# Where GpSimd writes the low words' integers while weights are converted: back into the raw chunk, or into two buffers of their own

## The chip, the core and the metric

The kernel runs on one core of a Trainium2 chip. It is measured in device microseconds from launch to end; the time shown is the median of three runs. One more execution was taken by the hardware profiler, and its times and trace are what the profile shows. Here TensorE (PE) multiplies matrices and writes to PSUM, VectorE (DVE) and ScalarE (ACT) work on PSUM and SBUF, GpSimd (POOL) works on SBUF, and SyncE (SP) issues most of the DMAs.

## The reference

Attention in which only keys within tau of each row's maximum count, then a feed-forward layer with a squared ReLU. Eight batches of eight heads, 576 rows, head size 64; the result is read as 4608 rows of 512.

```python
def _attn_ref(q, k, v, tau):                       # (8, 8, 576, 64) each, tau = 0.02
    scores = np.matmul(q, k.transpose(0, 1, 3, 2)) / np.sqrt(q.shape[-1])
    thresh = np.max(scores, axis=-1, keepdims=True) - tau
    scores = np.where(scores >= thresh, scores, -1000000000.0)
    scores = scores - np.max(scores, axis=-1, keepdims=True)
    attn = np.exp(scores)
    attn = attn / (np.sum(attn, axis=-1, keepdims=True) + 1e-09)
    return np.matmul(attn, v).astype(np.float32)

def _moe_ref(x, w_in, w_out):                      # (4608, 512), (512, 2048), (2048, 512)
    h = np.maximum(x @ w_in, 0.0)
    return (h * h @ w_out).astype(np.float32)
```

Queries, keys and values come as float32. The two weights come as float64, since they are drawn as float32 and then multiplied by a float64 scalar. The kernel multiplies in float32, so it converts the weights itself, and that is the work which the change touches.

## The kernel before

The kernel has three stages: attention (to about 510 us), the hidden layer and the output layer. Both layers multiply with 49 products of blocks in place of 64, from sums of blocks that VectorE and GpSimd make (the helpers at lines 121 to 125).

**Attention in periods.** The 32 pairs of heads are cut into 144 units of 128 query rows (`units`), and `period(p)` starts two of them, A = 2p and B = 2p + 1, while older ones are finished: the probabilities of period p - 1 are turned by TensorE and the outputs of period p - 2 multiplied with the values and sent out. Each unit has two heads, 0 and 1. The order of instructions in a period is written out by hand, in a list of steps; each engine works through its own instructions in the order in which the list gives them, and waits on semaphores for those of others. The steps that matter here, with the lines at which their instructions stand:

- VectorE: `topA0`, `topA1`, `topB0`, `topB1` (L452) copy a unit's scores from PSUM to SBUF and keep each row's maximum (the scores are negated, so it is a minimum); `maskA0` to `maskB1` (L467) compare the scores with the threshold, multiply with the exponentials and sum, and read two SBUF operands; `inv` (L477) makes reciprocals. The instructions named DVE_READ_ACCUMULATOR in the profile belong to the maxima and masks and write the row's number.
- GpSimd: `leastA` and `leastB` (L459) make a unit's thresholds from its maxima, 128x2 numbers; `over` (L474) and `xm` (L669) are small steps for the row sums and the outputs.
- ScalarE: `powA0` to `powB1` (L462) make the exponentials; `eU`, `eV`, `eW` (L523) and `eT` (L403, L411) copy what TensorE turned out of PSUM.

So a unit's mask waits for its threshold, which waits for both of its maxima.

**Weights in chunks.** 32 chunks of 128x512 float64 numbers (16 of the first weight and 16 of the second) are converted in periods 2 to 34, one chunk begun in each of periods 2 to 33 and finished in the one after. While this goes on the list `CONVERTING` gives the order:

```python
    CONVERTING = """
        s1 fetch SA T U c1 topA1 topA0 leastA eU SB over topB0 PV c2 powA1 powA0 maskA1
        powB0 topB1 c4 eT inv x V powB1 leastB maskA0 maskB0 c3 c5 eV W maskB1 c6 xm eW
    """.split()
```

On VectorE this makes the row topA1, topA0, topB0, maskA1, topB1, c4, inv, maskA0, maskB0, c5, maskB1, and on GpSimd leastA, over, c2, leastB, c3, c6, xm.

`fetch` brings a chunk by DMA into one of four raw buffers of 128x1024 32-bit words: each float64 is a low word and a high word beside each other, so `lo` and `hi` (`pick`) are views of every second word. The conversion then goes in six steps. `c1` (L205, ScalarE) takes the high words' absolute values as bits into a buffer `a`, one of three. `c2` (L212, GpSimd) multiplies the low words, read as unsigned integers, by 2^-29 and writes them as rounded integers from 0 to 8: the top three bits of the low word, rounded. `c3` (L219, GpSimd) bounds `a` to the range of exponents that float32 has. In the next period `c4` (L227, VectorE) shifts `a` by three bits, `c5` (L235, VectorE) joins it with the sign and the top of the exponent in `hi`, and `c6` (L245, GpSimd) adds the integers from `lo`; its result is the float32, written to the weights' tile for the first 16 chunks and to `a`, from where a DMA takes it to DRAM, for the others.

**Where the buffers lie.** One SBUF tile, `arena`, of 27264 float32 a partition is cut by hand. `Region` gives out places in a stretch of it: `tile` takes the next free stretch for a tag seen for the first time and turns round in its ring of buffers after that; `ring` sets the places of a tag by hand. The conversion's region `cv` is the last 6272 words of the arena, of which raw (4 x 1024) and `a` (3 x 512) take 5632; the first layer's input is loaded over it from period 40 on. The pieces of the second weight that are not among the 32 chunks would be converted later, by `convert_out`; with `EARLY` at 16 there are none.

Of the kernel before, what the change touches and what calls it, by code (L numbers as in the profile page):

```python
# [10 lines left out]
FP32 = mybir.dt.float32  # L11
I32 = mybir.dt.int32
U32 = mybir.dt.uint32
ALU = mybir.AluOpType
# [34 lines left out]
def kernel(  # L49
# [25 lines left out]
    nc = tc.nc  # L75
    B, H, S, D = q.shape
    P = 128
# [7 lines left out]
    BANK = 512  # L85
# [13 lines left out]
    ARENA = 27264  # L99
    X_SIZE = 7 * BANK + 3 * 7 * P  # L100
    X_AT = (ARENA - X_SIZE, ARENA - 2 * X_SIZE)
    arena = ctx.enter_context(tc.tile_pool(name="arena", bufs=1)).tile([P, ARENA], FP32, name="arena")
    sb, cv = Region(arena, 0, X_AT[0]), Region(arena, X_AT[0], ARENA)

    ident = const.tile([P, P], FP32, name="ident")
    make_identity(nc, ident)
# [46 lines left out]
    WC = 512  # L153
# [19 lines left out]
    raws, parts = {}, {}  # L173
# [34 lines left out]

    def convert2(m):
        if m in parts:  # L210
            lo = parts[m][0]
            nc.gpsimd.tensor_scalar(out=lo, in0=lo.bitcast(U32), scalar1=2.0**-29, scalar2=None, op0=ALU.mult)  # L212

    def convert3(m):
        if m not in parts:
# [403 lines left out]
    def period(p):  # L619
# [67 lines left out]
        def every(key):  # L687
# [7 lines left out]
            "SA": scored_a, "SB": scored_b,  # L695
            "PV": PV, "x": values_out, "xm": given_out,
            "c1": lambda: convert1(begun(p)), "c2": lambda: convert2(begun(p)),
            "c3": lambda: convert3(begun(p)), "c4": lambda: convert4(begun(p - 1)),
            "c5": lambda: convert5(begun(p - 1)), "c6": lambda: convert6(begun(p - 1)),
# [317 lines left out]
    with tc.manual_schedule():  # L1017
# [54 lines left out]
        def convert_out(n, tick):  # L1072
# [3 lines left out]
            for j, (i, (m, k, h)) in enumerate(mine):  # L1076
# [15 lines left out]
                if step == 0:  # L1092
                    b = b_pool.tile([P, BANK], FP32, tag="b", name="cw")[:, 0 : BANK // 2]
                    nc.scalar.activation(out=b, in_=hi.bitcast(FP32), func=AF.Abs)
                    parts[key] = (lo, hi, b.bitcast(I32))
                    convert2(key)
# [142 lines left out]
```

## Time and profile before

| | |
|---|---|
| runs | 1315.64, 1312.66, 1314.08 us; median 1314.08 |
| profiled execution | 1311.95 us, of which its span (first to last instruction) 1310.2 us |
| TensorE, whole span | 1265.7 us busy (97%) |
| VectorE | 1010.9 us (77%) |
| ScalarE | 845.5 us (65%) |
| GpSimd | 915.6 us (70%) |
| granted TensorE clock, mean | 0.997 |

The shares are means over stages that differ. In attention VectorE is nearly always busy, in the two layers TensorE. The conversion's own rows, over the whole run:

| step | engine, line | times | mean us of one |
|---|---|---|---|
| c1 | ScalarE L205 | 32 | 0.725 |
| c2 | GpSimd L212 | 32 | 2.064 |
| c3 | GpSimd L219 | 32 | 0.626 |
| c4 | VectorE L227 | 32 | 0.417 |
| c5 | VectorE L235 | 32 | 0.682 |
| c6 | GpSimd L245 | 16 + 16 | 1.477 and 1.478 |

The first c2 starts at 24.6 us and the last at 252.3 us; the last c6 starts at 263.5 us. After that the periods go on in the other order (`PLAIN`) to about 510 us. A row of the timeline gives start, length, engine, line, operation, and what is written and read with its shape; idle time of the engine just before it stands in brackets, with what ended it.

### The profile page before, as it was taken

How to read it: one execution, taken by the hardware profiler on the slowest of the kernel's cores; microseconds unless marked ns; L12 is line 12 of the kernel's file. 1: busy time of each engine (PE TensorE's matmuls, PEld its weight loads, DVE VectorE, ACT ScalarE, POOL GpSimd, SP SyncE). 2: the span in 40 equal slices, each digit the busy share in tenths (PEclk: the TensorE clock that was granted, in tenths of full speed). 3: DMA queues.
4: the chain of work that ended last, by engine and by line, in shares of the span. 5: the costliest groups of instructions: out<-in, count | busy, mean ns of one | idle time of the engine just before them, and what ended most of it. 6: DMA issues, size and time to landing. Idle time of an engine off the chain costs nothing.

```text
span 1310.2 us, 47769 instructions
## 1 busy us (share of the span) xinstructions
PE 1265.7 (97%) x19463; PEld 1140.1 (87%) x19463; DVE 1010.9 (77%) x2431; ACT 845.5 (65%) x1498; POOL 915.6 (70%) x1023
## 2 busy tenths in 40 slices
PE   8888888899999999999999999999999999999998
PEld 5666666677777777999999999999999999999998
DVE  6999999999999996877787778777646654665463
ACT  6999999888999985567756775665524332433240
POOL 2777777765555321877887888768777777777775
PEclk8999999999999999999999999999999999999999
DMA  6565666544433312466656665569644225522411
GB/s 159 140 158 138 165 176 192 143 103 98 98 78 83 79 42 62 142 199 193 203 176 202 207 193 170 189 242 395 241 161 162 60 104 161 162 64 99 161 33 34
DMA packets 247035, 192.12 MB, mean 147 GB/s; under 512 B 97184, under 2 KB 195488, under 8 KB 246816
## 3 DMA queue, kind: packets, MB, share of 16 engines
q1 hardware_dynamic: 245504, 188.66, 47.8%
q8 instruction: 153, 2.51, 0.8%
q14 instruction: 66, 0.54, 0.1%
q10 hardware_dynamic: 1312, 0.41, 0.1%
HBM read 116.65 MB, written 72.35 MB: 144 GB/s over the span
## 4 chain that ended last, share of the span: by engine, by line
PE 78%; ACT 4%; DVE 3%; DMA 1%; issue 1%; POOL 1%; ACTq 0%; DVEq 0%; POOLq 0%
PE ph L840 30%; PE po L975 27%; PE sc L532 7%; PE sc L434 6%; PE pt L380 4%; DVE arena L452 2%; PE sc L398 1%; ACT arena L523 1%; ACT arena L462 1%; PE sc L515 1%; DMA wall<-w 1%; DMA arena<-g 0%; DVE arena L125 0%; PE sc L380 0%; DVE arena L122 0%
## 5 line engine op out<-in xcount | busy, mean ns | idle before, releaser
L125 POOL TENSOR_TENSOR arena<-arena 128x512 f32<-128x512 f32 (+1 forms) x314 | 377.8, 1222 | 132.7 <-DVE arena L125 114.7
L975 PE MATMUL po<-wall,arena 128*128 128x128 f32 x3528 | 395.0, 275 | 1.5 <-ACT arena L752 1.4
L975 PEld LDWEIGHTS po<-wall,arena 128*128 128x128 f32 x3528 | 394.3, 192 | 2.1 <-ACT arena L752 1.8
L840 PE MATMUL ph<-arena,wall 128*128 128x128 f32 x3528 | 394.2, 275 | 0.7 <-DVE arena L659 0.7
L840 PEld LDWEIGHTS ph<-arena,wall 128*128 128x128 f32 x3528 | 394.0, 192 | 0.8 <-issue 0.8
L125 DVE TENSOR_TENSOR arena<-ph,arena 128x512 f32<-128x512 f32 x378 | 256.2, 688 | 86.4 <-PE ph L840 65.8
L122 POOL TENSOR_TENSOR arena<-arena 128x128 f32<-128x128 f32 (+2 forms) x314 | 255.2, 814 | 50.4 <-DMA arena<-w 34.2
L467 DVE SCALAR_TENSOR_TENSOR arena<-arena 128x576 f32<-128x576 f32 x288 | 239.6, 853 | 8.4 <-POOL arena L459 6.7
L125 DVE TENSOR_TENSOR arena<-po,arena 128x128 f32<-128x128 f32 x378 | 108.1, 289 | 167.8 <-PE po L975 163.5
L532 PEld LDWEIGHTS sc<-arena 64*64 64x64 f32 x5760 | 153.9, 133 | 82.3 <-DVE arena L452 68.7
L452 DVE TENSOR_SCALAR_CACHE_REDUCE arena<-sc 128x576 f32<-128x576 f32 x288 | 207.3, 747 | 10.5 <-ACT arena L523 3.8
L462 ACT ACTIVATE arena<-arena 128x576 f32<-128x576 f32 x288 | 208.9, 774 | 7.6 <-DVE arena L452 3.8
L786 ACT COPY c<-arena 128x512 f32<-128x512 f32 (+1 forms) x303 | 173.4, 579 | 50.2 <-DVE arena L122 41.3
L532 PE MATMUL sc<-arena 64*64 64x128 f32 (+1 forms) x5760 | 169.9, 262 | 27.1 <-DVE arena L452 26.9
L122 DVE TENSOR_TENSOR arena<-arena,c 128x512 f32<-128x512 f32 (+1 forms) x267 | 174.6, 662 | 6.1 <-ACT c L786 4.0
L434 PE MATMUL sc<-arena 64*64 64x64 f32 (+1 forms) x2304 | 172.7, 414 | 3.5 <-ACT arena L403 2.3
L523 ACT COPY arena<-pt 128x1024 f32<-128x1024 f32 x144 | 146.5, 1018 | 28.8 <-PE pt L380 27.8
L752 ACT COPY arena<-po 128x128 f32<-128x128 f32 x63 | 16.6, 264 | 186.5 <-PE po L975 183.7
L752 ACT COPY arena<-ph 128x512 f32<-128x512 f32 x63 | 36.6, 581 | 123.4 <-PE ph L840 122.9
L434 PEld LDWEIGHTS sc<-arena 64*64 64x64 f32 x2304 | 63.3, 134 | 48.6 <-issue 26.3
L380 PE MATMUL pt<-ident,arena 64*128 64x64 f32 x2304 | 101.1, 228 | 4.0 <-ACT arena L523 2.9
L459 POOL TENSOR_SCALAR arena<-arena,tau_p 128x2 f32<-128x2 f32 x144 | 62.8, 436 | 52.0 <-DVE arena L452 47.0
(51 smaller groups left out, 943.3 us busy)
## 6 DMA issues: line engine op xcount, KB each, us to landing
g<-arena SPq DMA_DIRECT2D x144, 256.0 KB, 2.6
arena<-g SPq DMA_DIRECT2D x144, 256.0 KB, 4.5
w<-arena SPq DMA_DIRECT2D x60, 256.0 KB, 2.5
wall<-w SPq DMA_DIRECT2D x49, 256.0 KB, 5.2
arena<-w SPq DMA_DIRECT2D x44, 256.0 KB, 3.3
arena<-in_v_dram SPq DMA_DIRECT2D x32, 288.0 KB, 4.0
out_dram<-arena SPq DMA_DIRECT2D x70, 128.0 KB, 2.2
arena<-in_q_dram SPq DMA_DIRECT2D x64, 128.0 KB, 3.7
```

The source lines that it names most:

```text
L122: e.tensor_tensor(out=out, in0=x, in1=y, op=ALU.subtract)
L125: e.tensor_tensor(out=out, in0=x, in1=y, op=ALU.add)
L380: made = nc.tensor.transpose(pt[:, r, ts(slot, HALF)], of[rows, :], ident[rows, rows])
L434: made = nc.tensor.matmul(sc[at, ds(to, count)], lhs, kT[rows, ds(at_k, count)], start=True, stop=True)
L452: made = nc.vector.tensor_scalar(out=s[:, j, :], in0=sc[:, ds(at, S)], scalar1=1.0, scalar2=None, op0=ALU.mult, op1=ALU.min, accum_out=nmx ...
L462: nc.scalar.activation(out=w[:, :, j, :], in_=of(j), func=AF.Exp, bias=nmx[:, j : j + 1], scale=-1.0)
L467: nc.vector.scalar_tensor_tensor(out=w[:, :, j, :], in0=of(j), scalar=thr[:, j : j + 1], in1=w[:, :, j, :], op0=ALU.is_le, op1=ALU.mult, a ...
L523: touch("weights", nc.scalar.copy(joined(to), whole(pt, 0, count)), at, 2 * BANK, m)
L532: made = nc.tensor.matmul(sc[ds(u * D, D), ds(5 * j * BANK + row, count)], loaded_v[i][rows, (c - (u != j)) % CH, :], wT[m][rows, ds(weigh ...
L786: nc.scalar.copy(c, y)
L840: nc.tensor.matmul(to[:, j, :], W_IN[m, k][:, ts(j, P)], of[k][:, m - 1, :], start=(not more and j == 0), stop=True, skip_group_check=True,)
L975: nc.tensor.matmul(to, g[:, j, :], w[:, j, :], start=(not more and j == 0), stop=(j == 3), skip_group_check=True)
```

## The change

The result of `c2` no longer goes back into the raw chunk, at every second word, but into a buffer `low` of 512 words in a row, one of two in turn, and `c6` reads it from there. For this the arena is made 512 words longer; the one buffer is this new end, the other the 512 words before it, which `cv` gives up (raw and `a` still fit in front of it). The number of instructions and their order on each engine stay; c2 gains a wait for the c6 that used the same buffer two chunks before.

```diff
-    arena = ctx.enter_context(tc.tile_pool(name="arena", bufs=1)).tile([P, ARENA], FP32, name="arena")
-    sb, cv = Region(arena, 0, X_AT[0]), Region(arena, X_AT[0], ARENA)
+    arena = ctx.enter_context(tc.tile_pool(name="arena", bufs=1)).tile([P, ARENA + BANK], FP32, name="arena")
+    sb, cv = Region(arena, 0, X_AT[0]), Region(arena, X_AT[0], ARENA - BANK)
+    cv.ring("low", [ARENA, ARENA - BANK])
...
     def convert2(m):
         if m in parts:
-            lo = parts[m][0]
-            nc.gpsimd.tensor_scalar(out=lo, in0=lo.bitcast(U32), scalar1=2.0**-29, scalar2=None, op0=ALU.mult)
+            lo, hi, a = parts[m]
+            low = cv.tile([P, WC], I32, tag="low", bufs=2, name="low")
+            nc.gpsimd.tensor_scalar(out=low, in0=lo.bitcast(U32), scalar1=2.0**-29, scalar2=None, op0=ALU.mult)
+            parts[m] = (low, hi, a)
```

## The prediction

> **What bounds the kernel now.** The change touches only GpSimd's work on the weight chunks, so I first asked the busy times of single stretches where that work lies (about 18 to 265 us) and which engine is full there. The columns are stretch and length, then busy us (instructions) of PE, PEld, DVE, ACT and POOL, the granted clock, the DMA share and GB/s.
>
> ```profile
> 100.00:140.00 40.00, 35.53 (x958) 25.62 (x950) 38.85 (x105) 37.18 (x68) 30.45 (x38) 1.00 0.55 146
> ```
>
> VectorE is busy for 38.85 of 40 us, ScalarE for 37.18, TensorE for 35.53 (its matmul ends are modelled), GpSimd for 30.45. VectorE sets the pace, and GpSimd matters only where VectorE waits for it. The view of waits, over 40 to 262 us, tells that (who waited, for whom: us in total, times, longest):
>
> ```profile
> PE sc L532 <- DVE arena L452: 26.0, 31, 0.9
> ...
> DVE arena L467 <- POOL arena L459: 5.7, 30, 0.2
> ACT arena L411 <- DVE arena L452: 4.9, 13, 0.4
> ```
>
> TensorE and ScalarE wait for VectorE's maxima; VectorE waits for one thing, 30 times, 0.19 us each: the threshold that GpSimd's L459 makes. The timelines of one period, GpSimd's first, then VectorE's (start us, us long), show why the threshold is late:
>
> ```profile
> 45.33 1.48 POOL L245 TENSOR_TENSOR wall<-arena 128x512 int32<-128x512 int32 x1 [1.37 <-DVE arena L235]
> ...
> 47.47 0.29 POOL L459 TENSOR_SCALAR arena<-arena,tau_p 128x2 f32<-128x2 f32 x1
> ...
> 48.16 2.08 POOL L212 TENSOR_SCALAR arena<-arena 128x512 int32<-128x512 uint32 x1
> 50.33 0.34 POOL L459 TENSOR_SCALAR arena<-arena,tau_p 128x2 f32<-128x2 f32 x1
> 50.63 0.61 POOL L219 TENSOR_SCALAR arena<-arena 128x512 f32<-128x512 f32 x1
> ```
>
> ```profile
> 45.10 0.80 DVE L467 SCALAR_TENSOR_TENSOR arena<-arena 128x576 f32<-128x576 f32 x1
> 45.84 0.08 DVE L467 DVE_READ_ACCUMULATOR arena<-arena 128x1 f32 x1
> ...
> 47.87 0.81 DVE L467 SCALAR_TENSOR_TENSOR arena<-arena 128x576 f32<-128x576 f32 x1
> 48.61 0.07 DVE L467 DVE_READ_ACCUMULATOR arena<-arena 128x1 f32 x1
> 48.61 0.75 DVE L452 TENSOR_SCALAR_CACHE_REDUCE arena<-sc 128x576 f32<-128x576 f32 x1
> ...
> 49.29 0.41 DVE L227 TENSOR_SCALAR arena<-arena 128x512 int32<-128x512 int32 x1
> ...
> 49.72 0.78 DVE L467 SCALAR_TENSOR_TENSOR arena<-arena 128x576 f32<-128x576 f32 x1
> 50.43 0.07 DVE L467 DVE_READ_ACCUMULATOR arena<-arena 128x1 f32 x1
> 50.70 1.15 DVE L467 SCALAR_TENSOR_TENSOR arena<-arena 128x576 f32<-128x576 f32 x1 [0.19 <-POOL arena L459]
> ```
>
> The threshold could run once the last maximum (48.61, ended by 49.36) is there, but it stands behind L212 in GpSimd's queue, which ends at 50.24; L459 starts at 50.33, and the third mask, ready to start at 50.43, starts at 50.70. L212 is thus on the loop that sets the period: the mask, VectorE's L235, GpSimd's L245, and round to L212 and L459, 7.28 us in all (L245 starts at 45.33 and again at 52.61).
>
> L212's 2.08 us are of two kinds. In the first two periods it takes 1.65 and 1.64 us. From then on it starts while a mask runs (47.87), a VectorE instruction with two SBUF inputs, and 48.61, where that mask's accumulator is read, plus 1.64 is its end. Another case agrees: at 252.26 it takes 2.23 us, and the mask before it ends at 252.85, plus 1.64 is 254.49. So L212 stands still for 0.45 us beside the mask, and its own work is 1.64 us.
>
> The third period shows what a threshold that is in time gives, since there L212 had run ahead of a late mask:
>
> ```profile
> 35.17 0.40 POOL L459 TENSOR_SCALAR arena<-arena,tau_p 128x2 f32<-128x2 f32 x1 [1.12 <-DVE arena L452]
> 35.54 1.13 POOL L219 TENSOR_SCALAR arena<-arena 128x512 f32<-128x512 f32 x1
> ```
>
> ```profile
> 36.13 1.16 DVE L467 SCALAR_TENSOR_TENSOR arena<-arena 128x576 f32<-128x576 f32 x1
> ```
>
> The third mask starts at 36.13, as soon as its forerunner's accumulator is read, but still takes 1.16 us instead of 0.80: L219, itself held by the mask before, runs beside it. From the last maximum's start (34.31) to L235 (37.22) it is 2.91 us; in the steady period 48.61 to 51.78, 3.17. The difference, 0.26 us, is what a threshold in time is worth.
>
> **The change part by part.** *L212's output.* It goes to a buffer in a row instead of every second word. No row shows this form. Bounds: 1.64 us, nothing gained, and 0.61, the L219 row, the same number of elements read once and written, in a row at both ends. The nearest row for integers is L245: it reads two int32 operands at every second word, writes in a row, and starts 0.51 us before the mask at 45.10 is done (45.84), so if it too is held, its own work is 1.48 - 0.51 = 0.97 us for twice the words that L212 reads. Reading every second word is therefore not what makes 1.64; left are the write at every second word and the conversion. I take 0.6 to 1.0, an estimate from these two rows. The price is the same for all of it: from 1.64 down, each 0.1 us moves the threshold 0.1 us ahead, until 0.26 is saved (1.38 us); below that VectorE no longer waits. Above 1.64 each 0.1 would cost 0.1.
>
> *L245's input.* One of its operands now lies in a row. Whatever this gives, L212 is held until 48.61 by the mask; it starts 0.45 us before, so L245 up to 0.45 longer, or shorter by any amount, costs and gains nothing here. If the mask came 0.45 earlier that cover would be gone, and L245 would count in full.
>
> *A wait moves.* The compiled order of instructions shows L212 taking a second wait, on GpSimd's own addition two chunks before (its buffer comes round again), while L245 loses its wait on GpSimd. That addition is done some 5 us before L212. A wait's own instruction takes 17 ns on GpSimd, before L212 inside the 0.45. Queued behind L212 is the threshold, for which the third mask waits, but the wait is over long before. All other instructions and DMA issues, on every queue, are as before, so nothing else is moved past anything.
>
> *What is late next.* With 0.26 off, the period is 7.02 us. ScalarE has little more room: it waits for the last maximum 0.38 us (L411, 4.9 us over 13 times) or 0.28 (L403) a period, so its own round is 6.90 to 7.00. It stays just under; if it took over it would cap the gain at 0.28, which is no less than what I count. TensorE has 0.9 (26.0 over 31).
>
> *Sum.* L212 runs 32 times; the first two periods are not steady, 30 wait (the 30 above). 30 x 0.26 = 7.8 us. The periods after it are VectorE's and the matrix products TensorE's, in the same order, so they shift by the whole. The profiled execution took 1311.95 us (span 1310.2), which becomes 1304.2. The median of the three runs is 1314.08, 2.13 above it; in its terms 1306.3.
>
> **The rivals.** *A, nothing changes.* The 1.64 us are the conversion between integer and float, whatever the layout. For it: VectorE's L227 at 49.29, 0.68 us after L212's true start, and the mask at 49.72 aren't held at all (0.41 and 0.78 us), though L219, working at full rate, holds a mask for 0.35. So L212's later part seems not to read, as if it worked on what it had. Against: L245 with integers is fast, though it converts nothing. Time: 1314. [...]
>
> *B, L212 speeds up a little*, by 0.03 to 0.2 us: 1 to 6 us, 1308 to 1313.
>
> *C, slower: L227 is held.* L212 writing at a steady rate may hold VectorE back for nearly its whole run, as L219 holds the mask, where now its later part lets L227 through. L227 is due 0.68 us after L212's true start. L219 runs from 50.63 to 51.24 and holds the mask from 50.70 to 51.05 (1.15 - 0.80), so it lets go 0.19 us before its end; a run of length x that does the same delays L227 by x - 0.87. Over 0.26, from x = 1.13, this is more than the threshold gains. At 1.2 it is 0.33 - 0.26 = 0.07 a period, 2.1 us; at 1.64, L227 0.77 late, the second mask starts at 50.49, L219 (50.63) is held until it ends at 51.21, and the third mask starts there instead of 50.70: 0.5 a period, 15 us. Time 1316 to 1329. For it: L219's hold on the mask. Against: L212 is just as long now and holds nothing. [...]
>
> **How the numbers follow.** Forecast 0.54: 1306, its own range 1305 to 1308. A 0.26: 1314. B 0.06. C 0.14: 1316 and up. Two runs of this kernel that differ by under 0.2% (2.6 us) can't be told apart. Faster is the forecast and two thirds of B: 0.58. Same is A and the rest of B: 0.28. Slower is C: 0.14. The range goes from 1304.5, ScalarE's cap with a little room, to 1316, which takes in A, B and C's near end.
>
> **What would show it.** Right: L212 under 1.85 us as shown (1.38 and the hold), the second L459 right after the last maximum, no waits of L467 for L459, the third mask still near 1.15, a period of 7.02, nothing different after the stage but its place. Wrong: L212 at 2.08 again (A); L227 over 0.41 (C); a period over 7.02 with L212 short and ScalarE without idle time, which would mean that ScalarE had less room than I read.

## The result, and the profile after

The changed kernel took 1322.04 us (median of three runs, 1320.92 to 1322.32) against 1314.08 before: a ratio of 1.0058, 95% interval 1.0035 to 1.0081. It became 8 us slower, where 8 us faster had been forecast. Its profiled execution took 1322.04 us, its span 1320.3. In its profile lines 205 to 219 have moved on by one to three, and later ones by three: the scaling (`c2`) is L214, the bounding of exponents (`c3`) L222, the joining (`c5`) L238, the addition (`c6`) L248, the threshold L462, the maximum L455, the mask L470. The ratios in this document leave out one execution of a kernel further down (the quick form in place), which took 5312.63 us where the other five took 1306 to 1311.

The stretch that was shown of before (columns as there):

```profile
100.00:140.00 40.00, 34.29 (x884) 24.83 (x882) 38.53 (x103) 36.28 (x65) 31.44 (x37) 1.00 0.53 141
```

VectorE (38.53 us for 38.85 before), ScalarE (36.28 for 37.18) and TensorE (34.29 for 35.53) do less in the same 40 us, GpSimd is busy for a microsecond longer (31.44 for 30.45): all go at the pace of something slower. The view of waits, again over 40 to 262 us, still has VectorE waiting for the threshold, 29 times for 0.19 us; what was to go away is there:

```profile
PE sc L535 <- DVE arena L455: 28.1, 30, 1.1
...
DVE arena L470 <- POOL arena L462: 5.5, 29, 0.2
```

One period on GpSimd, then the same on VectorE:

```profile
55.78 1.79 POOL L248 TENSOR_TENSOR wall<-arena 128x512 int32<-128x512 int32 x1 [1.31 <-DVE arena L238]
57.53 0.73 POOL L672 TENSOR_TENSOR arena<-arena 128x256 f32<-128x256 f32 x1
58.25 0.28 POOL L462 TENSOR_SCALAR arena<-arena,tau_p 128x2 f32<-128x2 f32 x1
...
58.92 1.98 POOL L214 TENSOR_SCALAR arena<-arena 128x512 int32<-128x512 uint32 x1
60.99 0.39 POOL L462 TENSOR_SCALAR arena<-arena,tau_p 128x2 f32<-128x2 f32 x1
```

```profile
58.39 0.07 DVE L455 DVE_READ_ACCUMULATOR arena<-sc 128x1 f32 x1
58.57 0.84 DVE L470 SCALAR_TENSOR_TENSOR arena<-arena 128x576 f32<-128x576 f32 x1
59.34 0.07 DVE L470 DVE_READ_ACCUMULATOR arena<-arena 128x1 f32 x1
...
60.45 0.78 DVE L470 SCALAR_TENSOR_TENSOR arena<-arena 128x576 f32<-128x576 f32 x1
61.16 0.07 DVE L470 DVE_READ_ACCUMULATOR arena<-arena 128x1 f32 x1
61.42 1.15 DVE L470 SCALAR_TENSOR_TENSOR arena<-arena 128x576 f32<-128x576 f32 x1 [0.19 <-POOL arena L462]
```

Three things are to be read here. The addition, which begins the row, takes 1.79 us where it took 1.48. What follows it comes later by that, so the *first* unit's threshold (58.25) ends at 58.53, and the first mask, ready at 58.39, starts at 58.57, 0.18 us late; before, it followed the maximum at once. And the scaling is hardly shorter: from 59.34, when the first mask lets it go, to 60.90 is 1.56 us, against 1.63 before, and the third mask comes 0.26 us after its forerunner all the same.

The scaling's 58.92 less the one at 51.43 makes a period of 7.49 us against 7.28. From the start of the first addition to that of the last it is 231.76 us (40.85 to 272.61) against 225.48, so the stage itself gives 6.3 us. Of the 10.1 us between the two profiled executions, another 2.8 is the start: ScalarE waited 4.2 us for the second chunk's DMA, before 1.4. That wait was anything from 2.6 to 6.2 us in the profiled executions of the kernels below, three of which have the chunk buffers of the kernel before, and the longest was in one of these, a kernel faster than before; so I don't count it to the change. The remaining 1.0 us lies behind the last addition and was not followed.

### The profile page after: what moved, and what is told of

Same layout as the page of the kernel before. It is cut to its first block, busy times and chain, and to the rows that moved or that the text cites. A ratio compares the mean times of both kernels' runs of the same rounds, so it can differ in the third digit from the quotient of the medians.

```text
span 1320.3 us, 47769 instructions
## 1 busy us (share of the span) xinstructions
PE 1269.5 (96%) x19463; PEld 1146.9 (87%) x19463; DVE 1014.6 (77%) x2431; ACT 845.3 (64%) x1498; POOL 923.0 (70%) x1023
## 4 chain that ended last, share of the span: by engine, by line
PE 73%; POOL 9%; issue 5%; ACT 4%; DMA 4%; DVE 3%; SPq 1%; POOLq 0%; ACTq 0%; DVEq 0%
PE ph L843 29%; PE po L978 27%; PE sc L535 6%; PE sc L437 6%; PE pt L383 4%; POOL arena L214 3%; POOL wall L248 2%; DVE arena L455 1%; ACT arena L526 1%; ACT arena L465 1%; POOL arena L462 1%; PE sc L401 1%; POOL arena L248 1%; POOL arena L222 1%; PE sc L518 1%
## 5 line engine op out<-in xcount | busy, mean ns | idle before, releaser
L470 DVE SCALAR_TENSOR_TENSOR arena<-arena 128x576 f32<-128x576 f32 x288 | 240.6, 856 | 13.9 <-POOL arena L462 6.6
L535 PEld LDWEIGHTS sc<-arena 64*64 64x64 f32 x5760 | 155.1, 134 | 88.0 <-DVE arena L455 71.1
L455 DVE TENSOR_SCALAR_CACHE_REDUCE arena<-sc 128x576 f32<-128x576 f32 x288 | 207.4, 747 | 11.7 <-ACT arena L526 4.3
L437 PEld LDWEIGHTS sc<-arena 64*64 64x64 f32 x2304 | 68.6, 134 | 45.3 <-issue 19.7
L462 POOL TENSOR_SCALAR arena<-arena,tau_p 128x2 f32<-128x2 f32 x144 | 64.5, 448 | 53.7 <-DVE arena L455 48.1
```

The lines of the kernel that those rows point to most:

```text
L437: made = nc.tensor.matmul(sc[at, ds(to, count)], lhs, kT[rows, ds(at_k, count)], start=True, stop=True)
L455: made = nc.vector.tensor_scalar(out=s[:, j, :], in0=sc[:, ds(at, S)], scalar1=1.0, scalar2=None, op0=ALU.mult, op1=ALU.min, accum_out=nmx ...
L470: nc.vector.scalar_tensor_tensor(out=w[:, :, j, :], in0=of(j), scalar=thr[:, j : j + 1], in1=w[:, :, j, :], op0=ALU.is_le, op1=ALU.mult, a ...
L535: made = nc.tensor.matmul(sc[ds(u * D, D), ds(5 * j * BANK + row, count)], loaded_v[i][rows, (c - (u != j)) % CH, :], wT[m][rows, ds(weigh ...
```

## The experiments

The first theory: the addition is dear in any layout in which its operands are not the two words of one raw pair (P), and its length moves the first threshold. Rivals: one operand in a row and the other not (M); the place of the buffers, or the longer arena (W).

**GpSimd alone.** The two instructions by themselves, eight times each, in several layouts, all on zeros.

```python
g.tensor_tensor(out=z, in0=hi, in1=lo, op=ALU.add)       # L76: words of the same chunk
g.tensor_tensor(out=z, in0=hi, in1=x, op=ALU.add)        # L78: high words and a row
g.tensor_tensor(out=z, in0=y, in1=x, op=ALU.add)         # L80: two rows
g.tensor_tensor(out=z, in0=hi, in1=lo2, op=ALU.add)      # L82: low words of another chunk
g.tensor_tensor(out=z, in0=y, in1=lo, op=ALU.add)        # L84: a row and low words
g.tensor_scalar(out=lo, in0=u(lo), **ops)                # L90: the scaling in place
g.tensor_scalar(out=x, in0=u(lo), **ops)                 # L94: into a row
g.tensor_scalar(out=f(x), in0=f(y), **ops)               # L98: float32, row to row
```

> This kernel leaves out the whole computation: it runs GpSimd's two instructions alone, eight times each, VectorE idle, on 128x512 elements, with operands in other layouts. Theory P (the two words of a pair): the addition is cheap when it reads the low and the high words of the same raw chunk, about 0.97 us by its own work (1.48 less 0.51 of standing still), and dearer by 0.25 us, 1.2 to 1.3, in every other layout: high words with a row, two rows, high words with low words of another chunk. Rival M (mixed steps): two rows and two views of different chunks are as cheap as one chunk, 0.97; only one view with one row costs 1.2 to 1.3. Rival W (where the buffers lie): all layouts cost the same here. The scaling of the low words: 1.64 us in place and 1.5 to 1.55 into a row, if the profiles' unheld first instructions (1.64 and 1.52) are its own work; about 0.61 for float32 in a row at both ends; if conversion makes the rest, unsigned row to integer row is near 1.5 as well.

The groups by line and form (total busy us, mean ns of one):

```profile
L90 POOL TENSOR_SCALAR raw<-raw 128x512 int32<-128x512 uint32 x8 | 12.2, 1531 | 0.7
...
L94 POOL TENSOR_SCALAR x<-raw 128x512 int32<-128x512 uint32 x8 | 12.1, 1508 | 0.6
L82 POOL TENSOR_TENSOR z<-raw,other 128x512 int32<-128x512 int32 x8 | 11.9, 1488 | 0.6
...
L98 POOL TENSOR_SCALAR x<-y 128x512 f32<-128x512 f32 x8 | 11.9, 1487 | 0.7
L78 POOL TENSOR_TENSOR z<-raw,x 128x512 int32<-128x512 int32 x8 | 10.3, 1288 | 0.6
L84 POOL TENSOR_TENSOR z<-y,raw 128x512 int32<-128x512 int32 x8 | 10.2, 1275 | 0.6
...
L80 POOL TENSOR_TENSOR z<-y,x 128x512 int32<-128x512 int32 x8 | 10.1, 1260 | 0.6
...
L76 POOL TENSOR_TENSOR z<-raw 128x512 int32<-128x512 int32 x8 | 8.3, 1037 | 5.9 <-DVE z L69 5.3
```

The idle time in the last line is that of the start. Both halves of the prediction's pricing fall with these rows. The scaling gains 23 ns from the row and not the 640 or more that were forecast, and converting isn't what takes it so long: float32 from row to row is 1487 ns as well. The addition goes from 1037 to 1288 ns as its operands leave the same chunk, which is M's and P's price for the change. W had all layouts cost the same here, and they don't. M is out too: two rows cost 1260, and two views with the same step of different chunks cost most of all.

**The integers at every second word of their own buffers.**

```diff
-            low = cv.tile([P, WC], I32, tag="low", bufs=2, name="low")
+            low = pick(arena[:, ds(ARENA - BANK, 2 * BANK)].bitcast(I32), m % 2)
```

> The changed kernel, but the two buffers are the even and the odd words of the same 1024 words, so the low words' integers are written at every second word again, though not in the raw chunk. Theory P (the addition is cheap only on the two words of one pair): the addition stays at 1.73 to 1.80 us, the scaling goes back to 1.64 of its own, the period stays at 7.5 us, time 1320 to 1324. Rival M (one operand in a row, the other not): the addition is back at 1.48, the period at 7.28, time 1312 to 1316. Rival W (where the buffers lie, or the longer arena): as P for the addition.

Ratio to before 1.0095 (1.008 to 1.011). GpSimd's timeline from one addition to the next, the first mask between them on VectorE, and the waits over 60 to 255 us:

```profile
100.26 2.01 POOL L248 TENSOR_TENSOR wall<-arena 128x512 int32<-128x512 int32 x1 [1.31 <-DVE arena L238]
...
107.97 2.00 POOL L248 TENSOR_TENSOR wall<-arena 128x512 int32<-128x512 int32 x1 [1.31 <-DVE arena L238]
```

```profile
103.27 0.84 DVE L470 SCALAR_TENSOR_TENSOR arena<-arena 128x576 f32<-128x576 f32 x1 [0.32 <-POOL arena L462]
```

```profile
DVE arena L470 <- POOL arena L462: 12.8, 51, 0.3
```

The addition takes 2.00 us, longer than either theory said (the time, 1326.67 us, lies above all three forecasts), but just what the instruction alone says: 1.49 in place of 1.29. The period is 7.71. And now the profile names the new wait: masks wait for thresholds 51 times, in the changed kernel 26 times over the same stretch, so the first mask waits in every period as well as the third.

**The other operand in a row**, the integers left in place (as the kernel before), and **both in a row** (as the changed kernel):

```diff
-            out=hi, in0=hi, scalar=-(1 << 30), in1=a, op0=ALU.bitwise_and, op1=ALU.bitwise_or
+            out=a, in0=hi, scalar=-(1 << 30), in1=a, op0=ALU.bitwise_and, op1=ALU.bitwise_or
...
+        hi = a
         nc.gpsimd.tensor_tensor(out=a, in0=hi, in1=lo, op=ALU.add)
```

> The kernel before, with the high part moved instead: VectorE's joining step writes its result over its other operand, in a row, and the addition reads this row and the low words' integers at every second word of the raw chunk. Buffers and arena are as before. Theory P: the addition goes to 1.73 to 1.80 us, the period to 7.5, time 1320 to 1324. Rival M: the same. Rival W (where the new buffers lie): the addition stays at 1.48, time 1312 to 1316.

> The changed kernel with the high part in a row as well, so that the addition reads two rows. Theory P: 1.73 to 1.80 us for the addition, period 7.5, time 1320 to 1324. Rival M (mixed steps): 1.48 or a little less, period 7.28 or less, time 1311 to 1316. Rival W: 1.73 to 1.80, for the buffers lie where they do in the changed kernel.

The first, without any new buffer, has a ratio of 1.0063 (1.0046 to 1.008), the second 1.004 (1.0027 to 1.0052; its 1319.06 us are a little under the forecast of P). The joining, which now writes in a row, still takes 0.68 us in both. Two additions following each other, of the one and of the other:

```profile
100.99 1.73 POOL L246 TENSOR_TENSOR wall<-arena 128x512 int32<-128x512 int32 x1 [1.37 <-DVE arena L235]
...
108.49 1.72 POOL L246 TENSOR_TENSOR wall<-arena 128x512 int32<-128x512 int32 x1 [1.37 <-DVE arena L235]
```

```profile
100.45 1.77 POOL L249 TENSOR_TENSOR wall<-arena 128x512 int32<-128x512 int32 x1 [1.31 <-DVE arena L238]
...
107.92 1.77 POOL L249 TENSOR_TENSOR wall<-arena 128x512 int32<-128x512 int32 x1 [1.31 <-DVE arena L238]
```

Periods of 7.50 and 7.47. W fails in the kernel too, since the first of these has no new buffer, and M fails with the second. Put together, the addition alone and the period rise together: 1.04 and 7.28 (before), 1.26 and 7.47 (both in a row), 1.28 and 7.50 (the high part in a row), 1.29 and 7.49 (the change), 1.49 and 7.71.

**The row alone.** The scaling writes into the row, but the addition reads from the chunk; it subtracts the high words from themselves, so the weights become zeros.

```diff
-            parts[m] = (low, hi, a)
...
-        nc.gpsimd.tensor_tensor(out=a, in0=hi, in1=lo, op=ALU.add)
+        nc.gpsimd.tensor_tensor(out=a, in0=hi, in1=hi, op=ALU.subtract)
```

> The changed kernel, in which the addition takes its operands from the raw chunk again: it subtracts the high words from themselves, so the weights become zeros and the low words' integers in the row are not used. So the scaling writes into a row and the addition reads pairs of words. Theory H (the second threshold stands still until the second mask is done, whenever the scaling ends within that mask): addition 1.48 us, scaling 1.56 of its own, period 7.28, time 1312 to 1316: the scaling's 0.1 us gain nothing. Rival L (as the prediction had it, each 0.1 us of the scaling moves the threshold by as much): period 7.19, time 1309 to 1312.

Ratio 1.0003 (0.9993 to 1.0012). The period on GpSimd, and the second and third mask on VectorE:

```profile
100.55 2.02 POOL L214 TENSOR_SCALAR arena<-arena 128x512 int32<-128x512 uint32 x1
102.67 0.39 POOL L462 TENSOR_SCALAR arena<-arena,tau_p 128x2 f32<-128x2 f32 x1
...
104.94 1.54 POOL L248 TENSOR_TENSOR wall<-arena 128x512 int32<-128x512 int32 x1 [1.31 <-DVE arena L238]
...
107.83 2.02 POOL L214 TENSOR_SCALAR arena<-arena 128x512 int32<-128x512 uint32 x1
```

```profile
102.11 0.78 DVE L470 SCALAR_TENSOR_TENSOR arena<-arena 128x576 f32<-128x576 f32 x1
102.83 0.07 DVE L470 DVE_READ_ACCUMULATOR arena<-arena 128x1 f32 x1
103.09 1.15 DVE L470 SCALAR_TENSOR_TENSOR arena<-arena 128x576 f32<-128x576 f32 x1 [0.19 <-POOL arena L462]
```

The period is back at 7.28 with the addition. The scaling ends at 102.57, which is 0.46 after the second mask began, 0.06 earlier than in the kernel before (50.24, 0.52 after 49.72). The threshold starts earlier by that, but takes 0.39 us instead of 0.34 and ends 0.23 after the mask (103.06; before, 50.67 after 50.43). So the threshold stands still while the mask runs, and the 0.06 by which it began earlier within the mask gained nothing. In the third period of before, where it began before the mask (35.17 and 35.41), it ended at 35.57 and the third mask didn't wait for it.

**The threshold before the scaling**, on the kernel before: GpSimd takes the bounding of the last chunk's exponents (`c3`) where the scaling was, then the second threshold, then the scaling.

```diff
-        ... over topB0 PV c2 powA1 powA0 maskA1
-        powB0 topB1 c4 eT inv x V powB1 leastB maskA0 maskB0 c3 c5 ...
+        ... over topB0 PV c3 powA1 powA0 maskA1
+        powB0 topB1 c4 eT inv x V powB1 leastB c2 maskA0 maskB0 c5 ...
...
-            "c3": lambda: convert3(begun(p)),
+            "c3": lambda: convert3(begun(p - 1)),
```

> The kernel before with GpSimd's order changed: the second threshold comes before the scaling of the low words, and the bounding of exponents moves to the next period, between the row sums and that threshold. Theory H: the third mask no longer waits for its threshold (0.26 us) and is held by the reads of the scaling in place of the bounding's (0.35), some 0.4: period 7.05 to 7.15, time 1306 to 1311. Rival R: the scaling holds the mask for its whole run, 1.5 us: period near 8, time above 1330.

Ratio 0.998 (0.9969 to 0.999), a period of 7.08 (additions at 99.45 and 106.53). The third mask:

```profile
104.55 1.21 DVE L467 SCALAR_TENSOR_TENSOR arena<-arena 128x576 f32<-128x576 f32 x1
```

It starts the moment the second ends, and the scaling holds it for 0.41 us (1.21 less 0.80), no longer, though after the second mask it goes on for 1.56 (104.55 to 106.11): H holds, R doesn't. The period is what was expected; the time is 2.6 us less than before where 30 x 0.20 is 6. The rest stays open. In this profiled execution, at 1313.37 us the longest of the ten, ScalarE waited 6.2 us for the second chunk's DMA, and three of the periods took 7.8 to 8.4 us; the other executions left no trace.

**What makes the scaling long.** The bounding of exponents takes 0.61 us, a multiplication 1.49: more forms of the same instruction, alone.

```python
g.tensor_scalar(out=f(x), in0=f(y), scalar1=1.0, scalar2=2.0, op0=ALU.min, op1=ALU.max)    # L78
g.tensor_scalar(out=f(x), in0=f(y), scalar1=1.0, scalar2=None, op0=ALU.min)                # L80
g.tensor_scalar(out=f(x), in0=f(y), scalar1=0.5, scalar2=None, op0=ALU.mult)               # L82
g.tensor_scalar(out=f(x), in0=f(y), scalar1=0.5, scalar2=1.0, op0=ALU.mult, op1=ALU.max)   # L84
g.tensor_scalar(out=f(x), in0=f(y), scalar1=0.5, scalar2=1.0, op0=ALU.mult, op1=ALU.add)   # L86
g.tensor_scalar(out=lo, in0=u(lo), scalar1=2.0**-29, scalar2=0.0, op0=ALU.mult, op1=ALU.add)  # L96
```

> This kernel leaves out the whole computation: GpSimd's tensor-by-number instruction alone on 128x512 elements, VectorE idle, in twelve forms, eight times each. In the first such kernel the multiplication took 1.49 to 1.53 us whatever the type and the layout, while the kernel's bounding of exponents, with two operations in one instruction (the smaller of, then the larger of), takes 0.61. Theory N (number of operations): every form with two operations takes about 0.6, every form with one about 1.5, and the low words in place take 0.6 to 0.65 when a second operation is named. Rival O (kind of operation): the smaller and larger of take 0.6 with one or two, a multiplication or an addition 1.5 with one or two.

```profile
L84 POOL TENSOR_SCALAR x<-y 128x512 f32<-128x512 f32 x8 | 15.3, 1918 | 0.7
...
L82 POOL TENSOR_SCALAR x<-y 128x512 f32<-128x512 f32 x8 | 11.9, 1488 | 0.7
L80 POOL TENSOR_SCALAR x<-y 128x512 f32<-128x512 f32 x8 | 11.9, 1484 | 0.7
L96 POOL TENSOR_SCALAR raw<-raw 128x512 int32<-128x512 uint32 x8 | 5.1, 639 | 0.7
...
L86 POOL TENSOR_SCALAR x<-y 128x512 f32<-128x512 f32 x8 | 4.9, 617 | 0.7
L78 POOL TENSOR_SCALAR x<-y 128x512 f32<-128x512 f32 x8 | 4.9, 613 | 5.4 <-DVE y L71 4.8
```

Neither theory holds as it stood. One operation costs 1.49, smaller of, multiplication and addition alike (1484 to 1489), but two cost 1.92 or 0.62, by the pair: (min, max) and (mult, add) are quick, (mult, max) and (add, max) slow. For the low words it means that naming an addition of zero takes the scaling from 1531 to 639 ns, in place.

**The quick form**, in the kernel before and in the changed one:

```diff
-            nc.gpsimd.tensor_scalar(out=lo, in0=lo.bitcast(U32), scalar1=2.0**-29, scalar2=None, op0=ALU.mult)
+            nc.gpsimd.tensor_scalar(out=lo, in0=lo.bitcast(U32), scalar1=2.0**-29, scalar2=0.0, op0=ALU.mult, op1=ALU.add)
```

> The kernel before, in which the scaling names a second operation, adding zero, so that it is the form that took 0.64 us alone in place of 1.53; it still writes in place. Theory H: the scaling stands still until the first mask is done and then takes 0.64, the second threshold runs before the second mask begins, the third mask no longer waits, period 7.02, time 1304 to 1308: what the prediction had counted for a scaling under 1 us. Rival E (ScalarE takes over): the third mask no longer waits, but the period stays at 7.1 to 7.2 and VectorE idles elsewhere, waiting for ScalarE: 1308 to 1312.

> The changed kernel with the same quick form of the scaling, so that it writes into a row. Theory H with P: the addition still takes 1.73 to 1.80, the first mask still comes 0.19 late after its threshold, and the third mask no longer waits: period 7.02 + 0.19 = 7.21, time 1310 to 1314, 5 to 7 us over the same form in place. Rival (the addition's length matters only behind a slow scaling): as the other kernel, 1304 to 1308.

In place: ratio 0.9962 (0.9949 to 0.9975), profiled execution 1306.19 us. GpSimd, VectorE, and the busy times of the stretch:

```profile
105.33 1.09 POOL L212 TENSOR_SCALAR arena<-arena 128x512 int32<-128x512 uint32 x1
106.64 0.40 POOL L459 TENSOR_SCALAR arena<-arena,tau_p 128x2 f32<-128x2 f32 x1 [0.23 <-DVE arena L452]
```

```profile
106.89 0.78 DVE L467 SCALAR_TENSOR_TENSOR arena<-arena 128x576 f32<-128x576 f32 x1
107.60 0.08 DVE L467 DVE_READ_ACCUMULATOR arena<-arena 128x1 f32 x1
107.60 1.15 DVE L467 SCALAR_TENSOR_TENSOR arena<-arena 128x576 f32<-128x576 f32 x1
```

```profile
100.00:140.00 40.00, 36.28 (x958) 25.59 (x956) 40.00 (x107) 38.28 (x70) 29.83 (x40) 1.00 0.58 151
```

The scaling is over at 106.42, the threshold now waits for the maximum and begins before the second mask (106.64 and 106.89), the third mask follows at once (107.60), and VectorE has no idle time left in this stretch (40.00 us busy of 40.00). The period is 7.02 (the joining at 101.67 and 108.69). This is the fastest of the kernels tried, under both of the pair compared here. Of the 30 x 0.26 = 7.8 us the ratio shows 5.0 (3.3 to 6.7) and the two profiled executions 5.8; the time, 1308.77 us, lies above H's 1304 to 1308 and within E's range, though the period is H's. The trace says where the rest is. From the first addition to the last it is 218.85 us against 225.48, 6.6 less, for two of the periods took 7.8 us: in each, VectorE waited for an exponential of ScalarE, as the waits over 60 to 255 us show. Another 1.2 us is the start, where ScalarE waited 2.8 us for the second chunk's DMA, before 1.4.

```profile
DVE arena L467 <- ACT arena L462: 1.2, 2, 0.6
```

In rows the same form gives 0.9994 (0.9986 to 1.0003) and a period of 7.23. GpSimd, then the first and the third mask on VectorE:

```profile
100.27 1.03 POOL L214 TENSOR_SCALAR arena<-arena 128x512 int32<-128x512 uint32 x1
...
104.36 1.80 POOL L248 TENSOR_TENSOR wall<-arena 128x512 int32<-128x512 int32 x1 [1.31 <-DVE arena L238]
...
107.50 1.02 POOL L214 TENSOR_SCALAR arena<-arena 128x512 int32<-128x512 uint32 x1
```

```profile
99.92 0.84 DVE L470 SCALAR_TENSOR_TENSOR arena<-arena 128x576 f32<-128x576 f32 x1
...
102.50 1.15 DVE L470 SCALAR_TENSOR_TENSOR arena<-arena 128x576 f32<-128x576 f32 x1
```

The third mask no longer waits: it starts as the second one's number is read. The first starts 0.18 us after the maximum before it is read (99.74), as in the changed kernel. So the layout costs the same 0.21 us a period behind a quick scaling as behind a slow one: it isn't paid through the scaling. From the first addition to the last the two differ by 6.7 us (225.52 and 218.85); the ratios are 4.2 us apart, a little under the 5 to 7 that were expected.

**How near the operands must lie.** The addition alone, both operands from one tensor, the second starting some words after the first.

> This kernel leaves out the whole computation: GpSimd's integer addition alone, 128x512, VectorE idle, both operands from one tensor at growing distances: in a row the second operand starts 0, 1, 2 and 4 words after the first; at every second word it starts 1, 1 (from an odd word), 2, 4 and 8 words after. Theory P (two words of one pair of 8 bytes): 1.04 us where both operands' words lie in the same pair each time (a row with itself, every second word with its neighbour at even start), 1.26 to 1.49 in all others. Rival D (nearness): everything up to 2 or 4 words apart takes 1.04, and only 8 words or another tensor is dearer. Rival T (same tensor): all take 1.04.

In a row, a start 0, 1, 2 or 4 words after cost 1037 ns each. At every second word:

```profile
L93 POOL TENSOR_TENSOR z<-raw 128x512 int32<-128x512 int32 x8 | 11.9, 1488 | 0.6
L91 POOL TENSOR_TENSOR z<-raw 128x512 int32<-128x512 int32 x8 | 9.1, 1142 | 0.6
L85 POOL TENSOR_TENSOR z<-raw 128x512 int32<-128x512 int32 x8 | 8.3, 1038 | 0.6
...
L89 POOL TENSOR_TENSOR z<-raw 128x512 int32<-128x512 int32 x8 | 8.3, 1037 | 0.6
```

L85 is one word apart, L89 two, L91 four, L93 eight. P falls in its letter, and D holds nearly as it stood: it isn't the pair but nearness, up to two words at this step (1037 and 1038 ns), with four in between (1142) and eight as dear as another chunk (1488 in both). So it does count where the operands lie, but relative to each other; W had meant the new buffers and the longer arena.

## Why the prediction was wrong, point by point

- **VectorE sets the pace, and its loop with GpSimd the period.** Right, and the third mask's wait for 0.26 us is worth what was counted in a period: without it the period is 7.02, as the sum had it. Over the stage that gave 6.6 us of the 7.8 (218.85 for 225.48).
- **The scaling at 0.6 to 1.0 us.** Wrong: 1.56 (1.98 with 0.42 of standing still), 1.51 alone. Two rows were taken as nearest that are other instructions: the bounding of exponents is one of the quick pairs of operations, the addition no scaling at all. Rival A's claim, that the layout doesn't matter to the scaling, was right but for 0.07 us, its reason, the conversion, wrong (alone and row to row, float32 takes 1487 ns as unsigned to integer does).
- **Each 0.1 us off the scaling moves the threshold by 0.1.** Wrong in this range. The threshold stands still beside the second mask (it ends 0.22 to 0.24 us after it in the kernel before, in the changed one and with the row alone), as the scaling does beside the first (0.42) and the bounding beside a mask in the third period (1.13 us for 0.61); that was read in those two and not applied to the third. 0.06 gained gave nothing (ratio 1.0003). From the third period, where the threshold had begun before the mask, the condition could have been read.
- **The addition up to 0.45 us longer costs nothing.** This is the step that made the kernel slower. The cover was worked out for the scaling, which waits for the first mask anyhow, but between the two in GpSimd's queue is the first unit's threshold, on which that very mask waits. Before it ended at 47.76 for a mask at 47.87, and 0.04 is what passes between them when the mask waits (58.53 to 58.57): the cover was 0.07 us. The addition grew by 0.25 of its own, 0.18 came through at the first mask, which itself takes 0.84 in place of 0.81, and that is the 0.21 a period, 6.3 us in 30 (what lengthens the mask by 0.03 no run here shows). Nor was its length priced: that two operands side by side could be the cheap case was not thought of.
- **A wait moves at no cost.** Right: the addition starts 0.06 us sooner for it (GpSimd idles 1.31 us before it, not 1.37), the scaling no later (0.08 us after the step in front of it ends, in both). But the addition two chunks before, which the scaling waits for, is the one that begins the same row and ends 1.35 us before it starts (57.57 and 58.92), not some 5.
- **ScalarE has 0.28 to 0.38 us of room.** Right in most periods: at 7.02 it doesn't hold VectorE up. In two it does, for 1.2 us together, which is where the sum, 30 times the same saving, was too large.
- **The rivals.** The measured 1322 lies in C's 1316 to 1329, but by chance: C, the only slower one, was the wrong mechanism, for the shift of the exponents (L230, which C had as L227) stays at 0.42 beside the scaling. B had the size of the scaling's gain (0.07 us), but that gain moved nothing. No rival had the addition.

## What to carry to other kernels

An instruction's cover must be followed through everything that stands behind it in its queue and not only to the next instruction that waits anyway; here a 0.28 us step between two long ones was the one that counted. A duration is borrowed only from a row with the same operation: where the row differs in one thing and costs half, that thing may be the whole of it. And a layout that looks untidy may be cheap for the reader (here 1.04 us against 1.26 to 1.49 for the addition alone): before words are moved apart, the consumer is to be priced too.

## What was not expected of the hardware

- GpSimd's instruction with a number, alone on 128x512 float32 from row to row: 1.49 us with one operation (the smaller of, a multiplication or an addition), 0.62 with (min, max) or (mult, add), 1.92 with (mult, max) or (add, max).
- GpSimd's addition, alone on 128x512: 1.04 us for operands up to two words apart at every second word and up to four in a row, 1.26 for rows of different tensors, 1.49 for two views at every second word of different chunks. Why nearness helps no run shows.
- The multiplication on the low words in place took 1.63 us in the kernel and 1.53 alone, where all words were zero; what makes the difference was not tried.
- With the threshold first, the scaling held the third mask for 0.41 us (1.21 less 0.80) of the 1.56 that it ran on (104.55 to 106.11), not for its length.
